# Attention scores copied out of PSUM in two vector operations with the minimum from both, a fixed PSUM tile, and more matrix products before the first input arrives

## The chip, the cores and the metric

The kernel runs on one core of a Trainium2 chip. That core has a matrix engine (PE, with its weight loads shown apart as PEld), a vector engine (DVE), a scalar engine (ACT), a general engine (POOL) and a queue that issues transfers (SP). Each has its own instruction stream, works in order, and waits for others through semaphores. Matrix products go to PSUM, 8 banks of 2 KB in each of 128 partitions; everything else lies in SBUF. The metric is the device time of one execution in microseconds (us).

## What is computed

Attention over 2 batches of 8 heads (1152 keys of width 64, queries averaged in pairs to 576), then a mixture of four two-layer networks over the 1152 rows of the attention output. Cut to what matters:

```python
q_pool = q.reshape(B, H, S // factor, factor, D).mean(axis=3)
scores = scale * np.matmul(q_pool, k.transpose(0, 1, 3, 2))
scores = scores - np.max(scores, axis=-1, keepdims=True)
attn = np.exp(scores)
attn = attn / (np.sum(attn, axis=-1, keepdims=True) + 1e-09)
...
for e in range(E):
    h = np.maximum(x @ w1[e], 0.0)
    out += p[:, e:e + 1] * (h @ w2[e])
```

## The kernel before, in words

The work has two stages. The first, attention, goes through 8 pairs of heads (`pairs`), and each pair through 9 tiles of 128 query rows by 1152 keys (`tiles`, 72 in all; tile 8 of a pair takes the last 64 rows of both heads). For one tile:

- `S_chunk` (L252): three chunks of 384 keys, each in a PSUM bank of its own, from two products each (three in tile 8). The three banks are one tile, `spt`, from a pool that holds one such tile (`ps_s`, L116).
- `neg_scores` (L255): one DVE operation reads all three banks, writes the negated, scaled scores to `sx` in SBUF, and gives the minimum of each row, `mn`, through its accumulator. In the profile it is a TENSOR_SCALAR_CACHE_REDUCE followed by a short DVE_READ_ACCUMULATOR.
- `exps` (L261): one ACT operation on `sx`, with `mn` as bias, which also gives the row sums.
- `T_chunk` (L269, L279, L281): nine transposes on PE in three groups of three, each group copied from PSUM to SBUF, the middle one by DVE, the others by ACT. These groups use the pool `ps_t`, four PSUM banks.
- `PV_part` (L294): products with the values into the one bank of `ps_o`.

The order is written by hand: the main loop at L415 issues, for tile g, the transposes of g, the exponentials of g+2, some preparation of the next pair (`prep_q`, L181 to L212; `prep_k`, L221), every second time a part of the value products, and then `scores(g + 3)`, that is three `S_chunk` and `neg_scores`. So between two groups of score products PE has one tile's transposes and, on most turns, something more. Since `spt` has one buffer, the score products of a tile come after the copy of the tile before.

`prep_q` for a later pair goes through ACT (L182, or L192 for the last rows) and then DVE (L183, L194); on ACT these stand behind an `exps`, and on DVE in front of a `neg_scores`.

Before any input has arrived, PE runs 14 transposes of the identity into a bank of `ps_o` (L347 to L349). Then come the preparation of the first pair (L350 to L366) and the main loop.

The second stage, the networks (L463 on), is a long run of matrix products, from about 299 us to the end.

Of the kernel before, what the change touches and what calls it, by code (L numbers as in the profile page):

```python
# [8 lines left out]
F32 = mybir.dt.float32  # L9
F32R = mybir.dt.float32r  # L10
AF = mybir.ActivationFunctionType
ALU = mybir.AluOpType
# [5 lines left out]
def attention_moe_kernel(ctx, tc, q, k, v, probs, w1, w2, out):  # L18
    nc = tc.nc
    B, H, S, D = q.shape  # L20
    NT, DM = out.shape
    E, _, FF = w1.shape
    P = 128
    HALF = 64
# [3 lines left out]
    NC = 384  # L28
# [3 lines left out]
    INV = 0.5 / float(D) ** 0.5  # L32
    NWARM = 14
    NX = 4

    const = ctx.enter_context(tc.tile_pool(name="const", bufs=1))
    ps_t = ctx.enter_context(tc.tile_pool(name="ps_t", bufs=4, space=PSUM))
    ident = const.tile([P, P], F32, name="ident")
# [18 lines left out]
    identr = const.tile([P, P], F32R, name="identr")  # L57
# [56 lines left out]
    with ExitStack() as actx:  # L114
        ap = actx.enter_context(tc.tile_pool(name="ap", bufs=1))
        ps_s = actx.enter_context(tc.tile_pool(name="ps_s", bufs=1, space=PSUM))  # L116
        ps_o = actx.enter_context(tc.tile_pool(name="ps_o", bufs=1, space=PSUM))
# [4 lines left out]
        sx = [ap.tile([P, S], F32, name=f"sx{i}") for i in range(NX)]  # L122
# [5 lines left out]
        ones = ap.tile([P, HALF], F32, name="ones")  # L128
        nc.gpsimd.memset(ones, 1.0)
        mn = [ap.tile([P, 1], F32, name=f"mn{i}") for i in range(NX)]  # L130
        sums = [ap.tile([P, NQT], F32, name=f"sums{i}") for i in range(2)]
        rs = [ap.tile([P, NQT], F32, name=f"rs{i}") for i in range(2)]
        pr = ap.tile([P, 2 * 9, E], F32, name="pr")
# [14 lines left out]
        def load_kv(dst, src, n, h0=0, h1=2):  # L148
            b, hp = pairs[n]
            nc.sync.dma_start(  # L150
                dst[:, h0:h1], src[b, 2 * hp + h0:2 * hp + h1].rearrange("h (p t) d -> p h t d", p=P))

        def add_q0(eng, t0, t1):
            eng.tensor_tensor(
                qs[:, t0:t1], qn[:, t0:t1, 0, :].unsqueeze(2).to_broadcast([P, t1 - t0, 2, D]),
                qn[:, t0:t1, 1, :].unsqueeze(2).to_broadcast([P, t1 - t0, 2, D]), ALU.add)
# [79 lines left out]
            for i in range(NQT):  # L236
                tiles.append((n, i))
        NTL = len(tiles)
        spt = {}

        def S_chunk(g, c):
            n, i = tiles[g]
            if c == 0:
                spt[g] = ps_s.tile([P, 3, 512], F32, tag="s", name="spt")
            cs = slice(c * NC, (c + 1) * NC)
            if i == 8:
                ops = [(q2m[n % 2][:, z, :], kab[:, y, cs]) for z, y in ((0, 0), (0, 1), (1, 0))]
            else:
                t, h = divmod(i, 2)
                ops = [(q2[n % 2][:, z, h, t * P:(t + 1) * P], k2[n % 2][:, h, cs]) for z in range(2)]  # L250
            for j, (w, x) in enumerate(ops):
                nc.tensor.matmul(spt[g][:, c, :NC], w, x, start=(j == 0), stop=(j == len(ops) - 1))  # L252

        def neg_scores(g):
            nc.vector.tensor_scalar(  # L255
                sx[g % NX].rearrange("p (c x) -> p c x", c=3), spt.pop(g)[:, :, :NC], -INV, None,
                ALU.mult, ALU.min, accum_out=mn[g % NX])

        def exps(g):
            n, i = tiles[g]  # L260
# [75 lines left out]
        def scores(g):  # L336
            if g < NTL:
                for c in range(3):
                    S_chunk(g, c)
                neg_scores(g)  # L340
# [3 lines left out]
        load_kv(kn, k, 0, 1, 2)  # L344
        load_q(0, 4, 9)
        load_kv(vn[0], v, 0)
        warm = ps_o.tile([P, 320], F32, tag="o", name="warm")  # L347
        for _ in range(NWARM):
            nc.tensor.transpose(warm[:, :P], ident, ident)  # L349
        add_q0(nc.vector, 0, 4)  # L350
        split_k0(0, 0, 4)
        split_k0(0, 4, 9)
# [62 lines left out]
        for g in range(NTL):  # L415
            n, i = divmod(g, 9)
# [141 lines left out]
```

## Time and profile before

| | |
|---|---|
| median of 3 runs | 687.91 us (687.35 to 691.38) |
| the profiled execution's own time | 686.83 us |
| its span, first to last instruction | 685.0 us |
| PE busy, share of the span | 670.9 us, 98% |
| DVE busy | 247.4 us, 36% |
| ACT busy | 244.9 us, 36% |
| DVE score copies (L255) | 72, mean 1357 ns |

Busy time is the time in which at least one instruction of an engine was in progress. The ends of matrix products are modelled, so that records of PE overlap a little. The slices of the page are 40 equal parts of the span, about 17 us each.

### The profile page before, as it was taken

The numbers are of one execution on the slowest core, as the hardware profiler recorded it, in microseconds if no ns is written. First come the engines' busy times: TensorE is split into PE (matmuls) and PEld (weight loads), VectorE is DVE, ScalarE is ACT, GpSimd is POOL, SyncE is SP. The second block draws the span as 40 slices with busy tenths as digits, with TensorE's granted clock in tenths as the row PEclk, the third lists the DMA queues.
The fourth block names the chain that finished last, engine by engine and source line by source line (L and its number), as shares of the span: only waits on it lengthen the run. The fifth ranks groups of instructions, "written<-read, shape, count | busy, mean of one in ns | idle before, by whom it ended". The sixth has DMA issues, their size and how long they took to land.

```text
span 685.0 us, 9821 instructions
## 1 busy us (share of the span) xinstructions
PE 670.9 (98%) x3986; PEld 580.6 (85%) x3986; DVE 247.4 (36%) x453; ACT 244.9 (36%) x474; POOL 201.4 (29%) x242
## 2 busy tenths in 40 slices
PE   7999999999999999999999999999999999999998
PEld 6878787877787877798989898989898989898987
DVE  6656565656565664321212121212121212121211
ACT  6767676767676766321111010101010202020200
POOL 3241414141414515293260080350170430310000
PEclk9999999999999999999999999999999999999999
DMA  7735262626262651022040030020030100001011
GB/s 214 196 70 167 69 173 63 179 57 184 52 194 76 160 156 32 32 95 90 1 123 0 1 97 26 28 96 0 1 124 0 36 28 0 1 1 31 16 42 51
DMA packets 26445, 50.74 MB, mean 74 GB/s; under 512 B 2464, under 2 KB 9888, under 8 KB 26400
## 3 DMA queue, kind: packets, MB, share of 16 engines
q1 hardware_dynamic: 26400, 50.12, 26.0%
q8 instruction: 31, 0.51, 0.3%
q14 instruction: 14, 0.11, 0.1%
HBM read 30.97 MB, written 2.36 MB: 49 GB/s over the span
## 4 chain that ended last, share of the span: by engine, by line
PE 95%; DVE 3%; issue 1%; ACT 0%; DMA 0%; SPq 0%; DVEq 0%
PE p L506 29%; PE p L94 27%; PE spt L252 14%; PE po L294 11%; PE pt L269 9%; PE p1t L94 3%; DVE sx L255 2%; PE pk L225 2%; PE pr L317 2%; DMA kn<-in_k_dram 0%; PE pq L199 0%; ACT sx L261 0%; DVE k L230 0%; ACT k L232 0%; ACT aT L281 0%
## 5 line engine op out<-in xcount | busy, mean ns | idle before, releaser
L94 PE MATMUL p<-xh,wslot 128*128 128x384 f32 x640 | 166.7, 339 | 0.0
L255 DVE TENSOR_SCALAR_CACHE_REDUCE sx<-spt 128x1152 f32<-128x1152 f32 x72 | 97.7, 1357 | 74.1 <-PE spt L252 72.6
L94 PEld LDWEIGHTS p<-xh,wslot 128*128 128x128 f32 x640 | 116.7, 188 | 0.4
L94 PE MATMUL p<-xl,wslot 128*128 128x384 f32 x320 | 108.3, 338 | 0.0
L261 ACT ACTIVATE sx<-sx,mn 128x1152 f32<-128x1152 f32 x72 | 90.8, 1261 | 14.4 <-DVE sx L255 14.0
L252 PE MATMUL spt<-k,q2all 128*128 128x384 f32 x384 | 84.8, 355 | 8.6 <-DVE sx L255 7.1
L281 ACT ACTIVATE aT<-pt 128x384 f32<-128x384 f32 x144 | 70.8, 491 | 55.4 <-PE pt L269 52.7
L252 PEld LDWEIGHTS spt<-k,q2all 128*128 128x128 f32 x384 | 64.1, 188 | 28.9 <-DVE sx L255 14.6
L269 PE MATMUL pt<-ident,sx 128*128 128x128 f32 x648 | 82.5, 272 | 0.0
L96 ACT ACTIVATE hb<-p 128x384 fp32r<-128x384 f32 x48 | 23.6, 493 | 159.9 <-PE p L94 159.9
L294 PE MATMUL po<-aT,vn 128*64 128x320 f32 (+1 forms) x576 | 77.6, 410 | 0.0
L269 PEld LDWEIGHTS pt<-ident,sx 128*128 128x128 f32 x648 | 75.2, 141 | 2.6 <-issue 0.4
L506 PE MATMUL p<-wslot,hb 128*128 128x512 f32 (+1 forms) x348 | 75.8, 375 | 0.0
L506 PEld LDWEIGHTS p<-wslot,hb 128*128 128x128 f32 x348 | 62.2, 188 | 11.7
L511 DVE SCALAR_TENSOR_TENSOR acc<-p,pw,acc 128x512 f32<-128x512 f32 (+1 forms) x28 | 20.5, 732 | 124.1 <-PE p L506 124.1
L294 PEld LDWEIGHTS po<-aT,vn 128*64 128x64 f32 x576 | 39.3, 137 | 28.3 <-issue 3.4
L96 ACT ACTIVATE k<-p 128x384 fp32r<-128x384 f32 x30 | 14.8, 492 | 130.6 <-PE p L94 130.6
L94 PEld LDWEIGHTS p<-xl,wslot 128*128 128x128 f32 x320 | 60.0, 188 | 0.4
L306 POOL TENSOR_TENSOR dg<-ident,rs 128x256 f32<-128x256 f32 x32 | 19.0, 615 | 125.7 <-DVE rs L304 125.7
L97 DVE SCALAR_TENSOR_TENSOR hb<-p,hb 128x384 fp32r<-128x384 f32 x48 | 26.8, 558 | 76.6 <-ACT hb L96 76.6
L100 POOL TENSOR_SCALAR wslot<-stg 128x512 fp32r<-128x512 f32 x12 | 7.5, 624 | 159.6 <-PE p L94 82.0
L506 PE MATMUL p<-wslot,k 128*128 128x512 f32 x168 | 51.9, 390 | 0.0
(103 smaller groups left out, 757.3 us busy)
## 6 DMA issues: line engine op xcount, KB each, us to landing
kab<-k SPq DMA_DIRECT2D x32, 288.0 KB, 4.8
q2all<-q2all SPq DMA_DIRECT2D x28, 256.0 KB, 4.8
vn<-in_v_dram SPq DMA_DIRECT2D x8, 576.0 KB, 6.8
kn<-in_moe_w_dram SPq DMA_DIRECT2D x8, 512.0 KB, 3.4
qn<-in_moe_w_dram SPq DMA_DIRECT2D x8, 512.0 KB, 3.3
stg<-in_moe_w_dram SPq DMA_DIRECT2D x8, 512.0 KB, 3.4
qs<-in_moe_w_dram SPq DMA_DIRECT2D x8, 512.0 KB, 3.3
qn<-in_q_dram SPq DMA_DIRECT2D x7, 576.0 KB, 6.3
```

What stands on the lines that cost most here:

```text
L94: nc.tensor.matmul(pt, w[:, a, kt, fs], x[:, kt, cols], start=(j == 0), stop=(j == last))
L96: nc.scalar.activation(hh[ft], pt, AF.Relu)
L97: nc.vector.scalar_tensor_tensor(hl[ft], pt, 0.0, hh[ft].bitcast(F32), ALU.max, ALU.subtract)
L252: nc.tensor.matmul(spt[g][:, c, :NC], w, x, start=(j == 0), stop=(j == len(ops) - 1))
L255: nc.vector.tensor_scalar(sx[g % NX].rearrange("p (c x) -> p c x", c=3), spt.pop(g)[:, :, :NC], -INV, None, ALU.mult, ALU.min, accum_out=m ...
L261: nc.scalar.activation(sx[g % NX], sx[g % NX], AF.Exp, bias=mn[g % NX], scale=-1.0, accum_out=sums[n % 2][:, i:i + 1])
L269: nc.tensor.transpose(pt[:, j, :], sx[g % NX][:, kt * P:(kt + 1) * P], ident)
L281: nc.scalar.activation(dst, src, AF.Copy)
L294: nc.tensor.matmul(po[h * HALF:(h + 1) * HALF, :w], vn[n % 2][:, h, kt, :], aT[grp][:, h, kt, :], start=(kt == 0), stop=(kt == KT - 1))
L306: nc.gpsimd.tensor_tensor(dg[:, h, :256].rearrange("p (j q) -> p j q", j=2), ident.unsqueeze(1).to_broadcast([P, 2, P]), r[:, h:4:2].unsqu ...
L506: nc.tensor.matmul(pc, h[ft][:, ts_], where[e, 2, ft // 4][:, a, ft % 4, c0:c1], start=(m == 0), stop=(m == len(ops) - 1))
L511: nc.vector.scalar_tensor_tensor(ac, pc, pw[:, tt, e:e + 1], ac, ALU.mult, ALU.add)
```

## The change: what it does

The score tile becomes one fixed PSUM tile of three banks, `sps`, allocated once in place of a pool tile for every `g`. The copy becomes two DVE operations, over chunks 0 and 1 (768 columns) and over chunk 2 (384), each with its own minimum into a column of `mn2`; a third, tiny DVE operation takes the smaller of the two into `mn`. The warm-up keeps its 14 transposes, now into a bank of `ps_t`, and adds 24 float32 products with 32 rows by 64 columns of the identity as weights (row groups in turn, both column halves) and 6 float32r products with 64 rows by 128 columns. All of these have 128 columns to stream.

```diff
+        mn2 = [ap.tile([P, 2], F32, name=f"mn2_{i}") for i in range(NX)]
+        sps = ps_s.tile([P, 3, 512], F32, name="sps")
...
-        spt = {}
...
-            if c == 0:
-                spt[g] = ps_s.tile([P, 3, 512], F32, tag="s", name="spt")
...
-                nc.tensor.matmul(spt[g][:, c, :NC], w, x, start=(j == 0), stop=(j == len(ops) - 1))
+                nc.tensor.matmul(sps[:, c, :NC], w, x, start=(j == 0), stop=(j == len(ops) - 1))
 
         def neg_scores(g):
-            nc.vector.tensor_scalar(
-                sx[g % NX].rearrange("p (c x) -> p c x", c=3), spt.pop(g)[:, :, :NC], -INV, None,
-                ALU.mult, ALU.min, accum_out=mn[g % NX])
+            x, m, m2 = sx[g % NX].rearrange("p (c x) -> p c x", c=3), mn[g % NX], mn2[g % NX]
+            for i, (c0, c1) in enumerate(((0, 2), (2, 3))):
+                nc.vector.tensor_scalar(x[:, c0:c1], sps[:, c0:c1, :NC], -INV, None, ALU.mult, ALU.min,
+                                        accum_out=m2[:, i:i + 1])
+            nc.vector.tensor_tensor(m, m2[:, 0:1], m2[:, 1:2], ALU.min)
...
-        warm = ps_o.tile([P, 320], F32, tag="o", name="warm")
+        warm = [ps_t.tile([P, P], F32, tag="t", name="warm") for _ in range(4)]
         for _ in range(NWARM):
-            nc.tensor.transpose(warm[:, :P], ident, ident)
+            nc.tensor.transpose(warm[0], ident, ident)
+        for _ in range(3):
+            for a in range(4):
+                for hh in range(2):
+                    r = slice(32 * a, 32 * a + 32)
+                    nc.tensor.matmul(warm[a][hh * HALF:(hh + 1) * HALF, :], ident[r, :HALF], ident[r, :],
+                                     start=True, stop=True)
+        for _ in range(3):
+            for a in range(2):
+                r = slice(64 * a, 64 * a + 64)
+                nc.tensor.matmul(warm[a], identr[r, :], identr[r, :], start=True, stop=True)
```

How the built program orders and holds these instructions is shown at three places; the brackets name the semaphores that an instruction waits for, by the engine that raises them (DMAHW is a transfer).

DVE in the first pair, before, from the score copy of tile 3:

```order
L255 TENSOR_SCALAR sx_97,mn_110<-spt 128x1152 [waits PE_49]
L279 COPY aT_98<-pt 128x3x128 [waits PE_49]
L183 TENSOR_TENSOR q2all<-pq,q2all 128x512 [waits Activation_49]
L255 TENSOR_SCALAR sx_94,mn_107<-spt 128x1152 [waits DVE_49,PE_49]
L279 COPY aT_98<-pt 128x3x128 [waits PE_49]
```

The same place now:

```order
L256 TENSOR_SCALAR sx_97,mn_3_114<-sps 128x768 [waits PE_49]
L256 TENSOR_SCALAR sx_97,mn_3_114<-sps 128x384
L258 TENSOR_TENSOR mn_110<-mn_3_114 128x1 [waits DVE_49]
L280 COPY aT_98<-pt 128x3x128 [waits PE_49]
L185 TENSOR_TENSOR q2all<-pq,q2all 128x512 [waits Activation_49]
L256 TENSOR_SCALAR sx_94,mn_0_111<-sps 128x768 [waits PE_49]
L256 TENSOR_SCALAR sx_94,mn_0_111<-sps 128x384
L258 TENSOR_TENSOR mn_107<-mn_0_111 128x1 [waits DVE_49]
```

One instruction became three. The first waits for PE, the second for nothing, and the third for DVE itself.

PE between the score products of tiles 3 and 4, as it stands now (before, the rows are the same with `spt` and other line numbers):

```order
L251 MATMUL sps<-k_0_77,q2all 128x384 [waits DVE_49]
L251 MATMUL sps<-k_0_77,q2all 128x384 x5
L270 MATMUL pt<-ident,sx_95 128x128 [waits Activation_49]
L270 MATMUL pt<-ident,sx_95 128x128 x2
L270 MATMUL pt<-ident,sx_95 128x128 [waits Activation_49]
L270 MATMUL pt<-ident,sx_95 128x128 x2
L270 MATMUL pt<-ident,sx_95 128x128 [waits DVE_49]
L270 MATMUL pt<-ident,sx_95 128x128 x2
L201 MATMUL pq<-ident,qs 128x128 [waits DVE_49,Pool_49]
L201 MATMUL pq<-ident,qs 128x128 x3
L251 MATMUL sps<-k_0_77,q2all 128x384 [waits DVE_49]
L251 MATMUL sps<-k_0_77,q2all 128x384 x5
```

Of the six score products of a tile the first waits for DVE, as before, and the other five have no wait.

PE at the program's start, now:

```order
L350 MATMUL warm<-ident 128x128 [waits Pool_49]
L350 MATMUL warm<-ident 128x128 x13
L355 MATMUL warm<-ident 64x128 x24
L360 MATMUL warm<-identr 128x128 [waits DVE_49]
L360 MATMUL warm<-identr 128x128 x5
L201 MATMUL pq<-ident,qs 128x128 [waits DVE_49,PE_49]
L201 MATMUL pq<-ident,qs 128x128 x3
L227 MATMUL pk<-identr,khl 128x128 [waits DVE_49,PE_49]
```

The 30 added products stand between the 14 transposes and the first transposes of queries and keys, which also wait for PE's own earlier products, since they take over the banks of the warm-up.

## Rows read from the trace of the kernel before

**Rows 1.** The page, its first two parts: busy time of each engine, and the granted clock of PE in 40 slices, in tenths.

```profile
PE 670.9 (98%) x3986; PEld 580.6 (85%) x3986; DVE 247.4 (36%) x453; ACT 244.9 (36%) x474; POOL 201.4 (29%) x242
...
PEclk9999999999999999999999999999999999999999
```

**Rows 2.** Windows: the start, the rest of the first pair's lead-in in two stretches, one pair in the steady part of attention, and the networks. After the stretch and its length come the busy time and the instructions of PE, PEld, DVE, ACT and POOL, the granted clock, the share of the transfers and their GB/s.

```profile
0.00:7.00 7.00, 5.24 (x30) 4.49 (x30) 3.11 (x6) 3.84 (x7) 1.51 (x11) 1.00 0.73 229
7.00:21.00 14.00, 11.10 (x74) 9.58 (x73) 9.61 (x17) 10.20 (x21) 7.71 (x7) 1.00 0.80 206
21.00:27.30 6.30, 5.08 (x40) 4.84 (x42) 5.02 (x8) 4.72 (x9) 0.00 (x0) 1.00 0.96 302
...
94.70:128.40 33.70, 33.18 (x244) 26.30 (x243) 20.10 (x39) 24.16 (x46) 10.31 (x13) 1.00 0.45 120
...
298.58:648.74 350.16, 350.16 (x1777) 321.70 (x1777) 71.61 (x118) 43.34 (x88) 98.58 (x105) 1.00 0.12 37
```

**Rows 3.** Waits: who waited for whom, us in total, times, longest.

```profile
PEld spt L252 <- DVE sx L255: 15.3, 27, 1.8
...
PE spt L252 <- DVE sx L255: 7.6, 13, 1.6
...
PEld pr L317 <- ACT aT L281: 1.5, 6, 0.3
```

**Rows 4.** Timeline of DVE in the fourth pair, without other engines' rows: start, duration, engine, line, operation, output and input.

```profile
95.04 0.17 DVE L303 TENSOR_SCALAR rs<-sums 128x4 f32<-128x4 f32 x1
95.24 0.18 DVE L304 RECIPROCAL rs<-rs 128x4 f32<-128x4 f32 x1
95.34 0.53 DVE L279 COPY aT<-pt 128x384 f32<-128x384 f32 x1
97.45 1.36 DVE L255 TENSOR_SCALAR_CACHE_REDUCE sx<-spt 128x1152 f32<-128x1152 f32 x1 [1.59 <-PE spt L252]
98.74 0.09 DVE L255 DVE_READ_ACCUMULATOR sx<-spt 128x1 f32 x1
98.74 0.55 DVE L279 COPY aT<-pt 128x384 f32<-128x384 f32 x1
99.21 0.68 DVE L230 CAST k<-pk 128x512 fp32r<-128x512 f32 x1
```

**Rows 5.** Timeline further on in that pair: score copies on DVE, the score products and the other PE work after them, and the ACT and DVE work between. The bracket is idle time of the engine just before, and what ended it.

```profile
105.25 1.36 DVE L255 TENSOR_SCALAR_CACHE_REDUCE sx<-spt 128x1152 f32<-128x1152 f32 x1 [2.36 <-PE spt L252]
...
106.65 1.27 ACT L261 ACTIVATE sx<-sx,mn 128x1152 f32<-128x1152 f32 x1
...
106.67 1.31 PE L252 MATMUL spt<-k,q2all 128*128 128x384 f32 x6 [0.46 <-DVE sx L255]
...
107.90 0.43 ACT L192 ACTIVATE q2all<-pq 64x64 fp32r<-64x64 f32 x2
...
108.37 0.46 DVE L194 TENSOR_TENSOR q2all<-pq,q2all 64x64 fp32r<-64x64 f32 x2 [1.29 <-ACT q2all L192]
108.86 1.36 DVE L255 TENSOR_SCALAR_CACHE_REDUCE sx<-spt 128x1152 f32<-128x1152 f32 x1
...
110.33 1.00 PEld L252 LDWEIGHTS spt<-k,q2all 128*128 128x128 f32 x6 [0.38 <-DVE sx L255]
...
111.69 1.36 DVE L255 TENSOR_SCALAR_CACHE_REDUCE sx<-spt 128x1152 f32<-128x1152 f32 x1 [0.27 <-PE spt L252]
...
115.40 1.01 PEld L252 LDWEIGHTS spt<-k,q2all 128*128 128x128 f32 x6 [0.49 <-issue]
...
116.78 1.36 DVE L255 TENSOR_SCALAR_CACHE_REDUCE sx<-spt 128x1152 f32<-128x1152 f32 x1 [3.25 <-PE spt L252]
...
118.20 0.99 PEld L252 LDWEIGHTS spt<-k,q2all 128*128 128x128 f32 x6 [0.28 <-DVE sx L255]
...
118.24 1.26 ACT L261 ACTIVATE sx<-sx,mn 128x1152 f32<-128x1152 f32 x1
...
119.50 0.58 ACT L182 ACTIVATE q2all<-pq 128x512 fp32r<-128x512 f32 x1
119.98 1.05 ACT L281 ACTIVATE aT<-pt 128x384 f32<-128x384 f32 x2
...
120.51 0.20 PEld L317 LDWEIGHTS pr<-dg,ones 128*64 128x64 f32 x4 [0.25 <-ACT aT L281]
...
124.70 1.36 DVE L255 TENSOR_SCALAR_CACHE_REDUCE sx<-spt 128x1152 f32<-128x1152 f32 x1 [0.28 <-PE spt L252]
...
126.12 1.01 PEld L252 LDWEIGHTS spt<-k,q2all 128*128 128x128 f32 x6
```

**Rows 6.** Timeline of the first 20 us: the warm-up, what follows it on PE, and score products in the first pair.

```profile
1.35 2.85 PEld L349 LDWEIGHTS warm<-ident 128*128 128x128 f32 x14 [1.35 <-POOL ident masks.py:199]
...
4.29 0.42 PEld L199 LDWEIGHTS pq<-ident,qs 128*128 128x128 f32 x4
...
4.99 0.60 ACT L182 ACTIVATE q2all<-pq 128x512 fp32r<-128x512 f32 x1
5.19 0.92 PEld L225 LDWEIGHTS pk<-identr,khl 128*128 128x128 f32 x9 [0.48 <-DVE khl L171]
...
9.25 0.69 DVE L230 CAST k<-pk 128x512 fp32r<-128x512 f32 x1
...
10.00 1.33 PE L252 MATMUL spt<-k,q2all 128*128 128x384 f32 x6 [0.98 <-DVE k L230]
...
12.78 1.34 PE L252 MATMUL spt<-k,q2all 128*128 128x384 f32 x6 [1.02 <-DVE sx L255]
...
20.21 0.69 DVE L183 TENSOR_TENSOR q2all<-pq,q2all 128x512 fp32r<-128x512 f32 x1 [1.44 <-ACT q2all L182]
```

**Rows 7.** Timeline, two other PE groups: value products into the two column halves (six products of the program, two records each), and ten float32r transposes.

```profile
98.16 1.19 PE L225 MATMUL pk<-identr,khl 128*128 128x128 f32 x10
...
102.41 1.47 PE L294 MATMUL po<-aT,vn 128*64 128x256 f32 x12
```

## The prediction

> **What bounds the kernel now.** I read the shares of the engines first [rows 1]: PE is busy 98% of the span, so what makes PE start later costs time, and what other engines do in PE's shadow costs nothing. PE's clock was granted at nine tenths or more in every slice, and 1.00 (the 2.4 GHz level) in each stretch of [rows 2]; there is no gate to lift. Then the windows [rows 2]: in the networks PE is busy for all of 350.16 us, so they neither absorb a delay nor shorten. A pair in the steady part of attention has 33.70 us with PE busy for 33.18; the lead-in is looser (11.10 of 14.00, 5.08 of 6.30). Then the waits [rows 3]: score products were released by the score copy 27 times. Yet only 7.6 us of that is idle PE; most of those waits fall where PE has hardly finished its other work. Last the timeline of one pair [rows 5], read for how long after the end of a copy the next score products load their weights: 106.61 to 106.67, 110.22 to 110.33, 118.14 to 118.20, 126.06 to 126.12. About 0.06 us is as fast as it gets, so three places of a pair hang on the copy itself and a fourth has some 0.05 us of slack; another, 113.05 to 115.40, has over 2 us. Three in each of six middle pairs are 18; the first pair has five (12.78 in [rows 6] is one) and the last four: the 27 of [rows 3].
>
> So the copy's latency is on the path at those places although DVE is busy a third of the time.
>
> **Part 1: one copy becomes two and a minimum.** A copy of 1152 columns takes 1.36 us, but what follows it starts 1.28 us after its start (97.45 to 98.74); a copy of 384 columns takes 0.55 and the next starts after 0.47 (98.74 to 99.21) [rows 4]. That is (1.28 - 0.47) / 768 = 1.055 ns per column. So 768 columns hold DVE for 0.47 + 384 x 0.001055 = 0.875 us, and the pair of operations ends at 0.875 + 0.47 + 0.08 = 1.425 us: 0.07 later than now. I call this d, the delay of the hand-over to PE. If the second waits until the first has ended, each costs its whole duration, 0.955 + 0.55 = 1.505, d = 0.15; if both reads of the accumulator (0.09 in [rows 4]) stand apart too, 1.685, d = 0.33. I take 0.07, because the row that is nearest, a score copy and the DVE copy behind it, shows the overlap.
>
> The minimum waits for DVE itself. L304 after L303 is such a pair: 0.03 us from one's end to the other's start, then 0.18 [rows 4]. So `mn` is ready 0.07 + 0.03 + 0.18 = 0.28 us later than now (e, the delay of the exponentials), and DVE's next instruction starts 1.425 + 0.03 + 0.10 - 1.28 = 0.27 later (95.24 to 95.34 is the 0.10).
>
> The Trainium skill, "VectorE: DVE Perf Modes", section "The DRAIN you can't avoid", says that the next operation does not start until the pipe has emptied, and to minimize the number of operations. By that rule d would be 0.15 and not 0.07. The rows speak against it as far as copies go, since the next starts 0.08 before the end.
>
> Does the hand-over get finer? The diff's index by bank suggests it, the built order does not: of the six products only the first waits for DVE, and the second copy has no wait of its own, so the first copy already waits for all six products, and the first product for both copies. I cost this at nothing gained.
>
> Now the sum, place by place, in a middle pair [rows 5]:
> - 106.67: waits for the copy, d = 0.07.
> - 110.33: its copy could not start before 108.86, behind L194, which waits for ACT L192, which stands behind the exponentials of 106.65. So it moves by e + d less the 0.06 of slack, together 0.29; 0.07 of it is already counted, so 0.22.
> - 118.20: 0.07. 126.12: 0.07.
> - 120.51: PEld waits for an ACT copy behind L182 and the exponentials of 118.24, six times in the run [rows 3]. These start 0.10 after their copy's end against 0.04 at 106.65, so they move by 0.28 - 0.06 = 0.22, of which PE has moved 0.07: 0.15.
>
> That is 0.58 us, times six pairs 3.5. In the first pair the second group of score products waits for L230, which is queued behind the first copy on DVE [rows 6]: 0.27. Its other five places give 5 x 0.07 = 0.35, and one of them follows L183, which waits for ACT behind the exponentials (20.21 in [rows 6]): 0.28 more. Together 0.9. The last pair has the 0.29 and three more places, 0.21: 0.5. **Attention: 3.5 + 0.9 + 0.5 = 4.9 us.** With d = 0.15 and e = 0.36 the same sum is 0.90 x 6 + 1.5 + 0.9 = 7.8; with d = 0.33 and e = 0.54 it is about 1.6 x 6 + 2.5 + 1.7 = 14. Were half of these waits swallowed by work that I took to be over, 2.5.
>
> The rest of DVE's added 0.27 per tile, 72 x 0.27 = 19 us, lies in its idle time; the tightest row that I found is the copy at 111.69, idle 0.27 before it. With less cover, one more place per pair would cost some 0.2.
>
> **Part 2: the warm-up.** Today the last weight load of the 14 transposes ends at 4.20 and the transposes of queries start at 4.29 [rows 6]: no room between. On them hang ACT L182 at 4.99, then the copies of keys behind it on ACT, then the first scores. The keys' transposes have 0.48 us of slack, the queries none. So what the 30 products take comes out later one for one, w. The first pair is a chain from there on (1.02 and 0.98 us of PE's idle time end with DVE work, not with a transfer), so it is not given back.
>
> No row has weights of 32 rows. The nearest is L294 [rows 7]: six products of the program with 256 columns in 1.47 us, in the two column halves at once; 0.24 each, so 0.12 with 128 columns. 24 x 0.12 = 2.9 us if the row groups run one after another; a quarter, 0.7, if all four run at once. The six float32r products cost 0.12 each by L225 (1.19 / 10), 0.7, or half in pairs. So w lies from 1.1 to 3.6. The lower end needs work on four row groups at once, which no row shows; the upper needs none, though the rows show it for column halves. Neither is nearer, and I take the middle, **2.3 us**. At half the clock it would double: the 14 transposes took 2.85 / 14 = 0.20 us each, L199's four 0.11. Since L199 stood right behind them at the full rate, I take the full rate.
>
> The Trainium skill, "TensorEngine Tiling (Array Packing)", section "Overview", calls the tiles independent. By that rule w would be at its lower end, 1.1, and the forecast 1.2 us less; no run here shows it yet.
>
> **The sum.** 4.9 + 2.3 = 7.2 us. On the profiled execution, 685.0 of span and 686.83 in all, that is 694.0; this execution lies 1.08 under the median of the runs, 687.91, so for the median about **695**.
>
> **The rivals.**
> - *The second copy is held until the first has emptied* (d = 0.15 or more): 7.8 to 14, with w 10 to 17, 698 to 705. Against it is the overlap in [rows 4]; for it, that no row has two operations with accumulators in a row. 22%.
> - *Cheaper than summed*: row groups run at once (1.1) and half the waits are swallowed (2.5): 3.6, 691.5. For it: of 15.3 us that PEld waited only 7.6 were idle PE. 19%.
> - *The banks do come back one by one*, on the other side. The first copy would start when two chunks are done, a third of 1.31 us = 0.44 earlier, and free two banks 0.955 later, 0.5 after the last product and not 1.36. The 7.6 us of idle PE would go, and with w 2.3 that gives 683. It decides by whether the third chunk's products and the second copy have waits of their own; the built order shows none. 6%.
> - The forecast, 5.5 to 9 us: 53%.
>
> **How the numbers follow.** The likeliest gives 695. For 8 in 10: below, the cheap case is taken in to 690.5, leaving 6% (banks one by one) and a bit; above, the held copy up to 702, leaving the dearest part. What a measurement here can tell from no change is about 1%, 6.9 us, and the forecast lies on that edge. Half of its chance (0.27) and nearly all of the held copy's (0.22) are slower by over 1%: 0.49. Within 1% are the rest of it (0.26), the cheap case (0.19), and a part of the banks' case (0.01): 0.46. Faster: 0.05.
>
> **What would show it.** The two copies should start 0.88 us apart and the pair end some 1.43 after its start; 0.96 or more says held. The exponentials should start about 0.3 later after the start of the copy. The wait of score products for the copy should grow from 27 cases, with idle PE up by several us in 10 to 270. L201's first transposes should start near 6.6 rather than 4.29; 5.4 says that the row groups ran at once. The networks should take 350.2 from their first product on, as now. Wrong would be: score products that start before the second copy has ended, or a lead-in that catches up with a transfer and gives w back.

## The result, and the profile after

The changed kernel takes 697.07 us (median of 4 runs, 695.43 to 698.1), the kernel before on the same chip 687.63: a ratio of 1.0123, with a 95% interval of 1.0082 to 1.0163. It is slower by about 9.4 us; 695.0 had been predicted, with a range of 690.5 to 702. By the time alone, 9.4 us stands between the forecast's own 5.5 to 9 and the 10 to 17 of the rival in which the second copy is held, so the time can't choose between the two; the rows below can. The profiled execution took 697.45, its span 695.6, against 685.0 before.

First the page of the changed kernel, its first two parts, which answer to [rows 1]:

```profile
PE 676.3 (97%) x4040; PEld 584.6 (84%) x4040; DVE 270.2 (39%) x669; ACT 241.3 (35%) x474; POOL 200.8 (29%) x242
...
PEclk8999999999999999999999999999999999999999
```

DVE has 216 more instructions (72 tiles, three for one and a second read of the accumulator) and 22.8 us more to do. Its share says nothing on the cost: 61% of the span is still idle. The first digit of the clock is new, and so windows of the changed kernel, with the columns of [rows 2]: the stretch in the lead-in that has the low clock, two pairs in the steady part, and a stretch of the networks.

```profile
13.00:20.00 7.00, 6.32 (x26) 5.73 (x24) 3.86 (x11) 3.12 (x8) 3.94 (x5) 0.52 1.02 233
75.80:110.40 34.60, 33.36 (x242) 26.33 (x242) 22.98 (x65) 23.64 (x47) 10.29 (x13) 1.00 0.44 117
110.40:145.00 34.60, 33.34 (x243) 26.30 (x242) 23.02 (x65) 23.65 (x47) 10.30 (x13) 1.00 0.44 116
309.00:659.00 350.00, 350.00 (x1777) 321.54 (x1776) 71.62 (x118) 43.32 (x88) 98.57 (x105) 1.00 0.12 38
```

A middle pair takes 34.60 us where it took 33.7, with as much PE work in it as before (33.36 against 33.18). The networks have PE busy all the time, as they had. So the time was lost in attention, and what was lost ahead of the networks stays lost. From the first score products of the second pair on, the steady part can be counted apart from the lead-in. They start at 41.12 now and at 36.34 before, so 4.78 us were lost by then; six middle pairs of 0.87 us give 5.2; the span grew by 10.6, which leaves 0.6 for the last pair.

The waits of the changed kernel, first PEld's, then PE's, which answer to [rows 3] (us in total, times, longest):

```profile
PEld sps L251 <- DVE sx L256: 17.9, 26, 2.1
...
PEld pr L318 <- ACT aT L282: 3.9, 6, 0.7
```

```profile
PE sps L251 <- DVE sx L256: 9.2, 19, 1.8
PE pr L318 <- ACT aT L282: 2.5, 6, 0.4
```

Idle PE behind the score copy grew from 7.6 to 9.2 us, and PE's own list now has a second line: six waits of 0.4 at `pr`, one in each middle pair, where before only PEld was seen waiting there. Of the two signs that the prediction named for these waits, one came and one did not: from 10 to 270 us PE was idle for 7.95 us before and is for 12.96 now, but PEld's waits for the score copy did not grow in number (27, now 26). PE's own did, from 13 to 19.

Timeline of the fourth pair, at its first tile, with DVE, PE and ACT:

```profile
111.78 0.96 DVE L256 TENSOR_SCALAR_CACHE_REDUCE sx<-sps 128x768 f32<-128x768 f32 x1 [2.09 <-PE sps L251]
...
112.66 0.55 DVE L256 TENSOR_SCALAR_CACHE_REDUCE sx<-sps 128x384 f32<-128x384 f32 x1
113.25 0.16 DVE L258 TENSOR_TENSOR mn<-mn 128x1 f32<-128x1 f32 x1
...
113.28 1.31 PE L251 MATMUL sps<-k,q2all 128*128 128x384 f32 x6 [0.54 <-DVE sx L256]
...
113.51 1.26 ACT L262 ACTIVATE sx<-sx,mn 128x1152 f32<-128x1152 f32 x1 [0.35 <-DVE mn L258]
```

The copies start 0.88 us apart, and the second ends 1.43 after the first began, as predicted (0.88 and 1.43). The score products start 1.50 after the first copy began, against 1.42 in [rows 5] (105.25 to 106.67): d is 0.08. They wait for both copies. The exponentials start 1.73 after it, against 1.40 and 1.46 before: e is 0.27 to 0.33.

### The profile page after: what moved, and what is told of

The parts are those of the page before. It is cut to its first block, busy times and chain, and to the rows that moved or that the text cites. A ratio compares the mean times of both kernels' runs of the same rounds, so it can differ in the third digit from the quotient of the medians.

```text
span 695.6 us, 10147 instructions
## 1 busy us (share of the span) xinstructions
PE 676.3 (97%) x4040; PEld 584.6 (84%) x4040; DVE 270.2 (39%) x669; ACT 241.3 (35%) x474; POOL 200.8 (29%) x242
## 4 chain that ended last, share of the span: by engine, by line
PE 87%; DVE 7%; ACT 3%; issue 2%; POOL 0%; ACTq 0%; DVEq 0%; POOLq 0%
PE p L517 28%; PE p L94 27%; PE sps L251 11%; PE po L295 9%; DVE sx L256 6%; PE pt L270 6%; PE p1t L94 2%; ACT sx L262 2%; PE pk L227 2%; PE pr L318 2%; ACT q2all L184 1%; DVE mn L258 1%; DVE q2all L196 1%; PE warm L350 0%; ACT q2all L194 0%
## 5 line engine op out<-in xcount | busy, mean ns | idle before, releaser
L256 DVE TENSOR_SCALAR_CACHE_REDUCE sx<-sps 128x768 f32<-128x768 f32 (+1 forms) x144 | 103.3, 755 | 58.1 <-PE sps L251 56.1
L251 PE MATMUL sps<-k,q2all 128*128 128x384 f32 x384 | 86.5, 360 | 11.7 <-DVE sx L256 8.6
L251 PEld LDWEIGHTS sps<-k,q2all 128*128 128x128 f32 x384 | 65.4, 191 | 32.9 <-DVE sx L256 17.1
L282 ACT ACTIVATE aT<-pt 128x384 f32<-128x384 f32 x144 | 68.2, 489 | 38.3 <-PE pt L270 36.6
```

What stands on the lines that cost most here:

```text
L251: nc.tensor.matmul(sps[:, c, :NC], w, x, start=(j == 0), stop=(j == len(ops) - 1))
L256: nc.vector.tensor_scalar(x[:, c0:c1], sps[:, c0:c1, :NC], -INV, None, ALU.mult, ALU.min, accum_out=m2[:, i:i + 1])
L282: nc.scalar.activation(dst, src, AF.Copy)
```

## The experiments

All ratios are to the kernel before on the same chip, with 95% intervals. They are worked out from all runs, and so differ a little from the ratio of two medians. The fixed tile in place of the pool's has no run of its own; at the tiles of a middle pair that wait for no copy, the steps from one group of score products to the next are the same before and now to within 0.03 us, which leaves it no visible cost.

**The copies and the minimum alone.** The warm-up is the one of before:

```diff
-        warm = [ps_t.tile([P, P], F32, tag="t", name="warm") for _ in range(4)]
+        warm = ps_o.tile([P, 320], F32, tag="o", name="warm")
...
-            nc.tensor.transpose(warm[0], ident, ident)
-        for _ in range(3):
...
-                nc.tensor.matmul(warm[a], identr[r, :], identr[r, :], start=True, stop=True)
+            nc.tensor.transpose(warm[:, :P], ident, ident)
```

> The two score copies and the minimum, with the warm-up of before. Theory (the later hand-over and the later exponentials cost about 0.87 us in each middle pair, the warm-up 2.25 us once, and a stretch at half the clock the rest): 0.87 x 6 and about 1.5 in the first and last pair, so 6.5 to 7.5 us slower than before, a middle pair of 34.6 us, no stretch at half the clock after the first 5 us. Rival (the longer attention comes from the warm-up or the clock and not from the copies): under 2 us slower and a pair of 33.7 us.

Measured: 695.02 us (4 runs) against 687.42, ratio 1.0109 (1.0077 to 1.0141). One middle pair runs from 72.78 to 107.42, 34.64 us, as expected. The time is 7.6 us over the kernel before, just above the 6.5 to 7.5 expected, so most of the 9.4 us comes from this half of the change. Its first pair shows no low clock, and its second pair starts at 38.12, 1.78 later than before.

**The warm-up alone.** The score copy is the one of before:

```diff
-            for i, (c0, c1) in enumerate(((0, 2), (2, 3))):
...
-            nc.vector.tensor_tensor(m, m2[:, 0:1], m2[:, 1:2], ALU.min)
+            nc.vector.tensor_scalar(
+                sx[g % NX].rearrange("p (c x) -> p c x", c=3), spt.pop(g)[:, :, :NC], -INV, None,
+                ALU.mult, ALU.min, accum_out=mn[g % NX])
```

> The 30 products in the warm-up, with the single score copy of before. Theory: the first transposes of queries start 2.25 us later and nothing gives it back, so 2.0 to 2.5 us slower while the clock is at its full rate; if a stretch at half the clock comes with this warm-up, up to 4 us and a granted clock under 1.000. Rival (the lead-in waits for transfers later on and swallows the delay): within 0.5 us of before.

Measured: 688.91 us (10 runs), ratio 1.0011 (0.9992 to 1.0030). The interval holds 1, so the time alone settles nothing; the timeline of PE's weight loads does more:

```profile
4.44 0.75 PEld L354 LDWEIGHTS warm<-ident 32*64 32x64 f32 x48 [0.25 <-issue]
5.36 0.41 PEld L359 LDWEIGHTS warm<-identr 64*128 64x128 f32 x6 [0.17 <-issue]
5.84 0.42 PEld L199 LDWEIGHTS pq<-ident,qs 128*128 128x128 f32 x4
```

The transposes of queries start at 5.84, 1.55 later than in [rows 6], and the difference of the medians is 1.5; 2.0 to 2.5 had been expected. The score products of the second pair start at 38.27 against 36.34 before, so the lead-in gives nothing back and the rival is out. Two halves of 7.6 and 1.5 make 9.1 of the measured 9.4. That the sum comes this near is in part luck: the changed kernel's lead-in has a stretch at the lower clock that the profiles of the halves don't have, and it lacks a held operation that the first half has there (both below).

**All 24 products on the same 32 rows** (one run; the score copy is the one of before). This asks whether four row groups really work at once:

```diff
-                r = slice(32 * a, 32 * a + 32)
+                r = slice(0, 32)
```

> The warm-up of the change with the score copy of before, but all 24 products take their weights from the first 32 rows, in place of the four row groups in turn (values that nobody reads). Theory (the four row groups work at once, since the 24 products went in three rounds): the 24 now go one row group after another, about 2.4 to 2.9 us in place of 0.7, and the first transposes of queries start 1.7 to 2.2 us later than with the four groups. Rival (the products are short because of issue or overlap on the columns alone): the same start within 0.3 us.

Measured: 691.02 us, with a stretch at the lower clock (granted clock 0.50 from 8.4 to 11.3 us), so that the time is not compared. The weight loads of PE before that stretch, at a granted clock of 1.00, to be read beside those of the kernel with only the warm-up changed, just above:

```profile
4.52 2.77 PEld L354 LDWEIGHTS warm<-ident 32*64 32x64 f32 x48 [0.33 <-issue]
7.46 0.41 PEld L359 LDWEIGHTS warm<-identr 64*128 64x128 f32 x6 [0.17 <-issue]
7.94 0.42 PEld L199 LDWEIGHTS pq<-ident,qs 128*128 128x128 f32 x4
```

The same 24 products took 2.77 us on one row group and 0.75 on four, and what follows started 2.10 later (7.94 against 5.84), both as expected. Row groups do work at once.

**No third operation.** From here on each edit is made to the kernel with the copies alone. The bias of the exponentials is the minimum of the second copy:

```diff
-            nc.vector.tensor_tensor(m, m2[:, 0:1], m2[:, 1:2], ALU.min)
...
-            nc.scalar.activation(sx[g % NX], sx[g % NX], AF.Exp, bias=mn[g % NX], scale=-1.0,
+            nc.scalar.activation(sx[g % NX], sx[g % NX], AF.Exp, bias=mn2[g % NX][:, 1:2], scale=-1.0,
```

> Two score copies and the warm-up of before, without the third DVE operation: the exponentials take the minimum of the last 384 columns as bias, so the true row minimum is left out (the shift cancels in the quotient but for the 1e-9). Theory (of the 0.87 us per pair only the places that hang on the copy itself, three times 0.07, are the hand-over; the rest comes through the exponentials, which start about 0.2 us later because of the third operation): a middle pair of 33.9 to 34.1 us, 2 to 3.5 us slower than before. Rival (the hand-over to the score products is most of it): a pair of 34.4 us or more, over 5 us slower.

Measured: 691.42 us (10 runs), ratio 1.0044 (1.0023 to 1.0066). The same place of one pair and the next, on PE:

```profile
71.22 1.31 PE L251 MATMUL sps<-k,q2all 128*128 128x384 f32 x6
...
105.22 1.31 PE L251 MATMUL sps<-k,q2all 128*128 128x384 f32 x6
```

A pair takes 34.00, as expected. The time is 4.0 us over the median of before, more than the 2 to 3.5 expected; five of the ten runs have a granted clock under 0.999, and the other five took 689.3 to 690.7, at most 3.3 over. So of the 0.87 to 0.9 us that a pair lost, 0.29 is the later hand-over of the PSUM tile (four places of 0.07), and the other 0.6 comes through the minimum and the exponentials that wait for it: the 128x1 operation costs twice what the split of the copy does.

**Two PSUM tiles.** The first copy hands back its two banks while the second still runs:

```diff
-        sps = ps_s.tile([P, 3, 512], F32, name="sps")
+        spa = ps_s.tile([P, 2, 512], F32, name="spa")
+        spb = ps_s.tile([P, 1, 512], F32, name="spb")
...
-                nc.tensor.matmul(sps[:, c, :NC], w, x, start=(j == 0), stop=(j == len(ops) - 1))
+                nc.tensor.matmul((spa[:, c, :NC] if c < 2 else spb[:, 0, :NC]), w, x, start=(j == 0), stop=(j == len(ops) - 1))
...
-                nc.vector.tensor_scalar(x[:, c0:c1], sps[:, c0:c1, :NC], -INV, None, ALU.mult, ALU.min,
+                nc.vector.tensor_scalar(x[:, c0:c1], (spb if i else spa)[:, :, :NC], -INV, None, ALU.mult, ALU.min,
```

> Two score copies, the minimum, and the warm-up of before, but with two PSUM tiles, one of two banks and one of one bank, so that each copy waits for its own products and hands back its own banks. Theory (what stood in the way was one tile for both copies): the first copy starts about 0.4 us before the last score product ends, score products wait for no copy in a middle pair, the pair takes 33.0 to 33.4 us, and the run is 2 to 6 us faster than before. Rival (DVE and ACT behind the copies set the pace, not the hand-over): no faster than before.

Measured: 688.75 us (10 runs), ratio 1.0007 (0.9988 to 1.0027); a middle pair takes 34.18. A miss: the hand-over is faster, yet the pair is slower than before. PE's waits, and then `pr` on PE's timeline, tell where the gain went:

```profile
PE pr L319 <- ACT aT L283: 7.7, 6, 1.3
PE spa L252 <- DVE sx L257: 3.4, 7, 2.4
```

```profile
91.90 0.76 PE L319 MATMUL pr<-dg,ones 128*64 128x320 f32 x4 [1.28 <-ACT aT L283]
```

PE waits 1.28 us for ACT in every middle pair. Further back stands the minimum. Two pieces of this kernel's timeline, POOL and then DVE:

```profile
83.55 1.27 POOL L164 TENSOR_TENSOR qs<-qn 128x512 f32<-128x512 f32 x1
...
88.09 1.44 POOL L178 TENSOR_TENSOR khl<-kn,khl 128x576 fp32r<-128x576 f32 x1
```

```profile
83.81 1.02 DVE L259 TENSOR_TENSOR mn<-mn 128x1 f32<-128x1 f32 x1
...
88.33 1.21 DVE L259 TENSOR_TENSOR mn<-mn 128x1 f32<-128x1 f32 x1
...
93.58 0.16 DVE L259 TENSOR_TENSOR mn<-mn 128x1 f32<-128x1 f32 x1
```

An operation on one column took 1.02 and 1.21 us in place of 0.16. It ended at 84.83 and 89.54; the POOL operations that were running when it began ended at 84.82 and 89.53. It looks held until POOL is done; the next experiment tests that. The Trainium skill, "SBUF — State Buffer", section "Who interferes with whom", states that DVE's second port pair is shared with GpSimd (POOL) under an exclusive lock, and that a DVE operation with two inputs in SBUF takes its second input through it and so contends with a GpSimd operation that reads SBUF. The trace agrees, with 1.02 and 1.21 against 0.16.

The changed kernel has the same, as its own timeline shows:

```profile
119.52 1.27 POOL L163 TENSOR_TENSOR qs<-qn 128x512 f32<-128x512 f32 x1
...
120.04 0.77 DVE L258 TENSOR_TENSOR mn<-mn 128x1 f32<-128x1 f32 x1
...
124.08 1.42 POOL L177 TENSOR_TENSOR khl<-kn,khl 128x576 fp32r<-128x576 f32 x1
...
125.13 0.38 DVE L258 TENSOR_TENSOR mn<-mn 128x1 f32<-128x1 f32 x1
...
125.61 1.26 ACT L262 ACTIVATE sx<-sx,mn 128x1152 f32<-128x1152 f32 x1 [0.48 <-DVE mn L258]
...
127.87 0.76 PE L318 MATMUL pr<-dg,ones 128*64 128x320 f32 x4 [0.43 <-ACT aT L282]
```

The minimum ends at 120.81 beside POOL's 120.79, and at 125.51 beside 125.50. The first has slack, as the step to the next score products is 5.08 us there and 5.07 before; the second delays the exponentials at 125.61, behind which ACT prepares what `pr` waits for.

**The minimum by an operation with one SBUF tensor.** The second minimum enters as a scalar per partition. The PSUM tile is one again:

```diff
-            nc.vector.tensor_tensor(m, m2[:, 0:1], m2[:, 1:2], ALU.min)
+            nc.vector.tensor_scalar(m, m2[:, 0:1], m2[:, 1:2], None, ALU.min)
```

> Like the scores alone, but the third operation has one tensor input from SBUF (the second minimum enters as a scalar per row) and not two. Theory (the minimum with two SBUF inputs is held until a running POOL operation with two SBUF inputs ends: 0.77 us at tile 2 and 0.38 at tile 3 of a pair where it is 0.16 elsewhere): the third operation takes 0.2 us or less at every tile, the wait of pr for ACT shrinks, a middle pair takes 34.3 us and not 34.6, and the run is 4.5 to 6 us slower than before, 1.5 to 2.5 less than the scores alone. Rival (the delay belongs to those places on DVE, whatever the operation): the same 0.77 and 0.38, the same pair of 34.6 us.

Measured: 694.86 us (4 runs) against 687.23, ratio 1.0100 (1.0069 to 1.0131); two of the runs with the clock at 1.00 all through took 693.4. In time this is a miss: 7.6 us slower than before (6.2 by those two runs) where 4.5 to 6 had been expected. A pair takes 34.50. All instructions of that line (duration in ns as min/median/max, first and last start in us), and then the timeline of one of them beside a POOL operation:

```profile
L258 DVE TENSOR_SCALAR mn<-mn x72: 212/214/216, 9.9 to 277.4; 128x1 f32<-128x1 f32 x72
```

```profile
86.08 1.41 POOL L177 TENSOR_TENSOR khl<-kn,khl 128x576 fp32r<-128x576 f32 x1
...
87.07 0.22 DVE L258 TENSOR_SCALAR mn<-mn 128x1 f32<-128x1 f32 x1
```

At 87.07 POOL still runs for 0.42 us, and the minimum takes 0.22: the holding is gone at all 72 tiles. With TENSOR_TENSOR the same line of the first experiment's kernel reads:

```profile
L258 DVE TENSOR_TENSOR mn<-mn x72: 158/159/1234, 9.9 to 278.7; 128x1 f32<-128x1 f32 x72
```

But the operation itself is 0.055 longer, which every exponential has to wait for, and the pair gets 0.14 shorter where 0.3 had been expected. The mechanism is shown; in this kernel, where the PSUM tile is handed back whole, the cure is worth little.

**Two tiles and this minimum together:**

```diff
+        spa = ps_s.tile([P, 2, 512], F32, name="spa")
+        spb = ps_s.tile([P, 1, 512], F32, name="spb")
...
+            nc.vector.tensor_scalar(m, m2[:, 0:1], m2[:, 1:2], None, ALU.min)
```

> Two PSUM tiles as in the run before with two tiles, and the minimum with one SBUF tensor input. Theory (with the hand-over bank by bank, what was left to wait for was the third operation, 1.02 and 1.21 us behind POOL at tiles 2 and 3): it takes 0.2 us or less, a middle pair goes from 34.2 to 33.2 to 33.5 us, and the run is 2 to 5 us faster than before. Rival (the exponentials on ACT set the pace there anyway): a pair of 33.9 us or more, no faster than before.

Measured: 681.89 us (4 runs) against 687.23, ratio 0.9906 (0.9879 to 0.9933): 5.3 us faster than before, with the true minimum of each row. That is a little more than the 2 to 5 expected. A middle pair takes 33.23, as expected. First its timeline, the second copy and the next tile's first weights, then the line of PE's waits:

```profile
105.49 0.55 DVE L257 TENSOR_SCALAR_CACHE_REDUCE sx<-spb 128x384 f32<-128x384 f32 x1
...
105.65 0.65 PEld L252 LDWEIGHTS spa<-k,q2all 128*128 128x128 f32 x4
```

```profile
PE pr L319 <- ACT aT L283: 1.7, 6, 0.3
```

PE loads weights for the next tile at 105.65, 0.39 before the second copy ends, and the wait at `pr` is 1.7 us in place of 7.7. Counted from the middle pair of the kernel with the copies alone (34.64), two tiles took off 0.46 us, the one-tensor minimum 0.14, and both together 1.41: each removes what hides the other's gain. The medians say the same (6.3, 0.2 and 13.1 us off 695.02), though runs at the lower clock have different shares in them.

**Two tiles and no third operation**, the bias from the first 768 columns; this edit is made to the kernel with two tiles:

```diff
-            nc.vector.tensor_tensor(m, m2[:, 0:1], m2[:, 1:2], ALU.min)
...
-            nc.scalar.activation(sx[g % NX], sx[g % NX], AF.Exp, bias=mn[g % NX], scale=-1.0,
+            nc.scalar.activation(sx[g % NX], sx[g % NX], AF.Exp, bias=mn2[g % NX][:, 0:1], scale=-1.0,
```

> Two PSUM tiles and no third operation: the bias is the minimum of the first 768 columns, so the last 384 are left out of the row minimum (the shift cancels in the quotient but for the 1e-9). Theory: exponentials wait for the second copy alone, a middle pair takes 33.0 to 33.3 us and the run is 4 to 6 us faster than before, the fastest so far. Rival: the third operation, once it is not held, was hidden, so no more than 0.5 us faster than the run with two tiles and the minimum by scalar.

Measured: 679.63 us (4 runs), ratio 0.9879 (0.9849 to 0.9909), a pair in 33.0. The pair is as expected, and the gain, 7.6 us, more than the 4 to 6 expected. A window of 33.00 us of this kernel:

```profile
109.00:142.00 33.00, 32.76 (x244) 26.26 (x243) 20.84 (x57) 23.05 (x48) 10.30 (x14) 1.00 0.46 123
```

PE is idle for 0.24 us of it, so there is hardly more to be had by handing PSUM back earlier. The third operation costs 2.3 us by the medians (681.89 against 679.63) even when nothing holds it, 0.23 of it in each middle pair.

## Why the prediction was right, and where it was off

The sign, and most of the size, came out by the steps that were given: attention loses time since PE waits for the score tile and DVE has to do more before it hands it back.

- *d = 0.07*: 0.08 measured. The second copy overlaps with the end of the first, so the rival that it is held until the first has emptied is refuted. The Trainium skill, "VectorE: DVE Perf Modes", section "The DRAIN you can't avoid", has the next operation start when the pipe has emptied, but goes on that a next operation that is not held starts earlier. The prediction left that second part out; the trace, with 0.88 where the first copy alone lasts 0.96, agrees with it.
- *e = 0.28*: 0.27 to 0.33 where nothing holds the minimum.
- *No finer hand-over*: right, as the score products still start after both copies. Two PSUM tiles are needed, and then the products do start early.
- *A middle pair, 0.58*: 0.87 to 0.9 measured. I compare the steps between the first score products of successive tiles, at the places of [rows 5], with the increment that the prediction gave in brackets: the step to 106.67 grew by 0.07 (0.07), to 110.33 by 0.27 (0.22), to 118.20 by 0.07 (0.07), to 126.12 by 0.08 (0.07). The rest is at 120.51, where `pr` waits for ACT. The weight loads of the changed kernel at 106.67, 110.33, 118.20 and the next tile, and then those of that next tile before:

```profile
113.27 1.00 PEld L251 LDWEIGHTS sps<-k,q2all 128*128 128x128 f32 x6 [0.77 <-DVE sx L256]
117.20 1.00 PEld L251 LDWEIGHTS sps<-k,q2all 128*128 128x128 f32 x6 [0.64 <-DVE sx L256]
...
125.15 0.99 PEld L251 LDWEIGHTS sps<-k,q2all 128*128 128x128 f32 x6 [0.36 <-DVE sx L256]
...
130.71 1.00 PEld L251 LDWEIGHTS sps<-k,q2all 128*128 128x128 f32 x6 [0.49 <-DVE aT L280]
```

```profile
123.35 1.00 PEld L252 LDWEIGHTS spt<-k,q2all 128*128 128x128 f32 x6 [0.49 <-issue]
```

  The step from 118.20 to the next score products, 5.15 us, became 5.56. **This is the term that was mis-sized: 0.15 predicted, 0.41 measured**, six times. There the minimum took 0.38 in place of 0.16, held by POOL, which is 0.22. Without the third operation the step is 5.15 as before, so all of it comes through that operation. With the one-tensor minimum it is 5.40 (87.09 to 92.49), 0.25 over before: the 0.15, the 0.055 by which that operation is longer, and some 0.05 more. Here as at 110.33 I had subtracted about 0.06 of slack that the runs don't show; the 0.10 between a copy and its exponentials isn't slack. I had looked for work queued behind the minimum on DVE, and not for what its two SBUF inputs share with POOL.
- *The first pair, 0.9*: 1.78 in the kernel with the copies alone. Of this, 0.36 is there at the first score products (6.78 against 6.42 in the kernel before), ahead of any score copy: ACT's first work on keys, which waits for a transfer, starts 0.27 later in that profile (4.53 against 4.26). Another part is the second tile's minimum, which took 1.23 up to the end of a POOL operation at 14.79:

```profile
13.58 1.23 DVE L258 TENSOR_TENSOR mn<-mn 128x1 f32<-128x1 f32 x1
```

  With the one-tensor minimum the offset is 1.36 (37.70 against 36.34), 0.42 less, and 0.29 of it is there at the first score products. That leaves 1.07 for the copies and the minimum, near the 0.9.
- *The warm-up, 2.3*: 1.5 alone. The mechanism is that of the lower end, four row groups at once, and its products took what it gave (0.75 and 0.41 us against 1.1 in all), but gaps where the weights' shape changes come on top (0.25, 0.17 and 0.07 us in the kernel with only the warm-up changed), which the prediction put at nothing. The Trainium skill, "TensorEngine Tiling (Array Packing)", section "Overview", has the tiles independent: the trace agrees, 0.75 against 2.77 us. In the changed kernel's own profile these products took longer, and the transposes of queries, L201, start at 6.54, 2.25 later than the first transposes in [rows 6]:

```profile
4.52 1.18 PEld L355 LDWEIGHTS warm<-ident 32*64 32x64 f32 x48 [0.33 <-issue]
6.03 0.44 PEld L360 LDWEIGHTS warm<-identr 64*128 64x128 f32 x6 [0.33 <-issue]
6.54 0.42 PEld L201 LDWEIGHTS pq<-ident,qs 128*128 128x128 f32 x4
```

  So the 2.3 looks right there, but by luck and not for the reason given; why the loads of the same products took 1.18 in one profile and 0.75 in the other, both at a granted clock of 1.00, isn't settled.
- *The clock*: I took the full rate throughout. The ground that I gave for it, a transpose of the warm-up at 0.20 us against 0.11 for L199, is not the clock by the rows: [rows 2] has 1.00 from 0 to 7 us, over both. And the full rate did not hold: the changed kernel's profile has a stretch at the 1.2 GHz level (granted clock 0.52 from 13 to 20 us). On its timeline, the second, third and fourth group of score products:

```profile
12.51 1.93 PE L251 MATMUL sps<-k,q2all 128*128 128x384 f32 x6 [1.57 <-DVE k L232]
...
15.98 2.29 PE L251 MATMUL sps<-k,q2all 128*128 128x384 f32 x6 [0.68 <-DVE sx L256]
...
19.93 1.29 PE L251 MATMUL sps<-k,q2all 128*128 128x384 f32 x6
```

  From the first to the third of these it takes 7.42 us. In the kernel with the one-tensor minimum it takes 5.70 (10.74 to 16.44), with the clock at 1.00; there, as in the changed kernel, no minimum is held at this place. So the low clock costs about 1.7 us in this profile. (With the copies alone it is 6.07, of which 0.37 is the held minimum of 13.58.) The changed kernel's one execution with the clock at 1.00 on the mean took 695.43, the other three (0.995 to 0.997) 696.68 to 698.1; executions of the kernel before differ in the same way, 687.19 at 1.00 and 688.96 at 0.997 on one chip.

Put together, the 10.6 us by which the span of the changed kernel's profile grew are these, with the prediction's terms in brackets: 1.95 for the warm-up, as the first score products start at 8.37 against 6.42 (2.3); 1.7 for the low clock (nothing); 1.1 for the rest of the first pair (0.9); 5.2 for the six middle pairs (3.5); and 0.6 for the last (0.5). So two steps fell short, each by about 1.7 us: the six middle pairs, nearly all of it at `pr`, and a clock taken as full. The execution at 1.00 is 8.2 us over one of the kernel before at 1.00 (687.19), and the prediction, which was made for the full rate, has 7.2. That it comes so near is in part luck, since the warm-up was put too high by 0.4 to 0.8 and the pairs too low.

## What to carry to other kernels

Splitting a copy gains only if its consumer waits for the parts: look in the order for the wait, and give each part a tile of its own. A tiny operation that is put between a producer and its consumer costs more than its columns, and its form matters: with two SBUF tensors as inputs on DVE it can last until a POOL operation that happens to run has ended, with one tensor and a per-partition scalar it does not. When one wait is taken away and nothing is gained, read the waits again before giving the idea up: here the second one hid the whole gain of the first.

## What was not expected

- A 128x1 operation on DVE took 0.16 us at most tiles and 0.38, 0.77, 1.02, 1.21 or 1.23 at others, up to 1.32, to within 0.03 of the end of a POOL operation. That operation need not have two tensor inputs itself: in the changed kernel the minimum at 19.79 took 0.62, to 20.41, beside a TENSOR_SCALAR on POOL that ended at 20.40.
- Twenty-four float32 products with 32x64 weights took 0.75 us on four row groups and 2.77 on one.
- The granted clock fell to the lower level for some 7 us in the lead-in although PE had been busy for 3.82 of the 6 us before and was for 6.32 of those 7; in the kernel before, PE was busy for 3.86 of the same 6 us and its clock stayed at 1.00. The kernel with the 24 products on one row group has such a stretch too (0.50 from 8.4 to 11.3 us), with the score copy of before. What brings it is open; no run was made to find out.
